# Loading half of a weight by a pattern of eight: fused cross-covariance attention and mixture-of-depths MLP

## The chip, the cores and the metric

The kernel runs on one core of one Trainium2 chip. The metric is the device time of one execution in microseconds (us); the median of three runs before the change is 258.89 us (258.16 to 259.0). A core has TensorE (PE, with its weight loads PEld), VectorE (DVE), ScalarE (ACT), GpSimd (POOL), SyncE (SP), and sixteen DMA engines that move data between HBM and the on-chip memory SBUF. SBUF has 128 partitions. Matmuls write to PSUM.

## The reference

Two stages, for four batches of N = 6208 tokens with C = 256 channels, all float32:

```python
qn = q / (norm(q, axis=1) + 1e-6)            # over the tokens
kn = k / (norm(k, axis=1) + 1e-6)
a  = softmax(kn^T @ qn / tau)                # 256 x 256 per batch
x  = v @ a
scores = x @ w_gate                          # one per token
idx    = the 128 tokens of a batch with the highest scores
h  = relu(x[idx] @ w1)                       # w1: 256 x 1024
ye = h @ w2                                  # w2: 1024 x 256
out = x;  out[idx] = x[idx] + sigmoid(scores[idx]) * ye
```

The 1024 columns of w1 and the 1024 rows of w2 are the MLP's units. A unit is column i of w1 and row i of w2; in which order the units are summed doesn't matter, as long as both weights use the same order.

## The kernel before

**Tiles and order.** A batch is cut into six chunks of 1024 tokens (8 rows on each of 128 partitions) and a rest of 64 tokens. For each batch the kernel loads the q and k chunks, then the v chunks. GpSimd issues these loads (lines 187 and 189, in `emit_load`); they are cast to bf16 on the way, so a load of 1 MB from HBM fills 512 KB of SBUF. Per q/k chunk TensorE adds to three accumulators: k^T q (line 303) and the Gram matrices of q and of k (lines 305 and 307). At the end of a batch's q and k come the norms and the softmax; then v is transposed (line 403), the scores are formed (line 440), and the output is formed (line 474), copied to a staging buffer (line 482, ScalarE) and stored by SyncE (line 491, in `emit_store`, 1 MB per chunk). The selection of 128 tokens is a search for a threshold on VectorE. The selected rows of v are gathered by an indirect DMA (line 603), run through attention and MLP again (`h_ps` line 646, `y_ps` line 660), and scattered over the output (line 697).

**What sets the order.** The program writes the order of the work out by hand. While it is built, a planner keeps a clock per engine (`vt_clock`) and a model of the two DMA queues (`Rings`), and at each step picks what is ready: a step of a selection or MLP chain, a score, an output, or the next input row. Loads are issued by `pump` as buffers come free, at most four not yet landed by the planner's model. On the chip each engine works through its instructions in the order written and waits on semaphores.

**The DMA queues.** GpSimd's loads go through a software queue (q0 in the profile), SyncE's weights and stores through a hardware queue (q1). Both are served by the same sixteen engines. A DMA of 128 partitions is dealt out over the sixteen, eight partitions to each. When an engine has done its share it writes a 4-byte packet, the completion; a load has landed when all sixteen are there.

**The weights (lines 215 to 226 and 845 to 854).** At the start SyncE loads w1 and w2 in float32 into two of the staging buffers, `w1_st` and `w2_st`, and the gate's vector into `wg_row`. Partition p of `w2_st` gets the eight rows 8p to 8p+7 of w2, so w2's unit order is "unit 8p + fc is row p of block fc". ScalarE casts both to bf16, and the cast of w1 sorts its columns into the same blocks:

```python
nc.sync.dma_start(out=w2_st, in_=moe_w2.rearrange("(p fc) d -> p fc d", p=P))
...
w1v = w1_st.rearrange("p a c -> p (a c)").rearrange("p (dc m fc) -> p dc fc m", dc=C // P, fc=NFC)
for dc in range(C // P):
    nc.scalar.copy(w1_sb[:, dc, :].rearrange("p (fc m) -> p fc m", fc=NFC), w1v[:, dc])
nc.scalar.copy(w2_sb, w2_st)
```

Then a small matmul and a copy spread the gate's vector over the partitions (lines 850 to 852). w1 and w2 are first used by the MLP of the first batch; w2 also serves as operand of matmuls that only keep TensorE busy (`idle`, line 841).

Of the kernel before, what the change touches and what calls it, by code (L numbers as in the profile page):

```python
# [18 lines left out]
P = 128  # L19
# [8 lines left out]
def kernel(  # L28
# [12 lines left out]
    nc = tc.nc  # L41

    B, N, C = q.shape
# [6 lines left out]
    NFC = F // P  # L50
# [101 lines left out]
    def now():  # L152
        return vt_clock["pe"]
# [49 lines left out]
    def pump():  # L203
        rings.run(now())
        flying[:] = [key for key in flying if rings.done.get(key, 1.0e9) > now()]
        while nxt_unit[0] < len(units):
            u = units[nxt_unit[0]]
            if in_use[bucket(u)] >= limit[bucket(u)] or len(flying) >= AHEAD:
# [6 lines left out]
    w1_sb = const.tile([P, C // P, F], BF16)  # L215
# [3 lines left out]
    w1_st = st_pool.tile([P, RPP, C], F32, name="stage")  # L219
    w2_st = st_pool.tile([P, RPP, C], F32, name="stage")  # L220
    nc.sync.dma_start(out=w1_st.rearrange("p a c -> p (a c)").rearrange("p (dc f) -> p dc f", dc=C // P),
                      in_=moe_w1.rearrange("(dc p) f -> p dc f", p=P))
    nc.sync.dma_start(out=w2_st, in_=moe_w2.rearrange("(p fc) d -> p fc d", p=P))
    nc.sync.dma_start(out=wg_row, in_=moe_w_gate[None, :])
    rings.add(1, 2.0, UNIT, "w1")
    rings.add(1, 2.7, UNIT, "w2")
# [566 lines left out]
    def stage_ready():  # L793
        if len(stage_keys) < ST_BUFS:
            return 0.0
        key = stage_keys[-ST_BUFS]
        if key in stage_free:
            return stage_free[key]
        return rings.landing(("st",) + key) + 0.3
# [43 lines left out]
    while True:  # L843
        pump()
        if not cast_done and now() > 8.0:
            w1v = w1_st.rearrange("p a c -> p (a c)").rearrange("p (dc m fc) -> p dc fc m", dc=C // P, fc=NFC)
            for dc in range(C // P):
                nc.scalar.copy(w1_sb[:, dc, :].rearrange("p (fc m) -> p fc m", fc=NFC), w1v[:, dc])
            nc.scalar.copy(w2_sb, w2_st)
            wg_ps = ps_m.tile([P, 512], F32, name="m_ps")  # L850
            nc.tensor.matmul(wg_ps[:, 0:C], lhsT=ones_f[0:1, :], rhs=wg_row, start=True, stop=True)
            nc.scalar.copy(wg_bcast, wg_ps[:, 0:C])
            vt_clock["act"] = max(vt_clock["act"], now()) + 4.5
            cast_done = True
# [9 lines left out]
        if eat_at < len(eat):  # L864
            kind, u, x = eat[eat_at]
            if u in loaded:
                row = x if kind == "p1" else x[1]
                r = rings.landing(arrival_key[u + (int(row >= RPP // 2),)]) + 0.1
                if acc_dead[0]:
                    r += -0.7 if u == ("v", L, LAST) else 0.7  # L870
                if kind == "p1":
                    if u[2] == FIRST and x == 0:
                        r = max(r, acc_free[0])
                else:
                    r = max(r, min(vt_bank)) if vt_live < VT_BUFS or acc_dead[0] else FAR
# [5 lines left out]
        if out_at < len(outs):  # L881
            b, g, pr = outs[out_at]
            if b in a_ready and (b, g) in vts and score_at > gs.index(g) + b * len(gs) and (
                    (b, g[0]) not in late or hot):
                r = max(a_ready[b], vt_ready[(b, g)], min(o_bank))
                if g[0] < NFULL and g[1] == 0 and pr == 0:
                    r = max(r, stage_ready())
                if eat_at < len(eat) and eat[eat_at][0] == "p1" and b == E and r < t + 1.0:
                    arr = able[-1][0] if able and able[-1][1] == 2 else FAR
                    if max(r, t) < arr < max(r, t) + 0.5:  # L890
                        r = FAR
# [10 lines left out]
        if fit:  # L902
            r, prio, what = min(fit, key=lambda a: (a[1], a[0]))
# [5 lines left out]
        else:  # L909
            r, prio, what = min(able, key=lambda a: (a[0], a[1]))  # L910
# [122 lines left out]
```

## Time and profile before

| | |
|---|---|
| median of 3 runs | 258.89 us (258.16 to 259.0) |
| the profiled execution | 257.59 us, its span 255.9 us |
| granted TensorE clock, mean | 0.977 of full |
| PE busy | 214.0 us (84%) |
| PEld busy | 187.4 us (73%) |
| ACT busy | 106.5 us (42%) |
| DVE busy | 92.4 us (36%) |
| POOL busy | 56.9 us (22%) |
| HBM read, written | 78.91 MB, 25.95 MB: 410 GB/s over the span |
| chain that ended last | DMA 60%, PE 26%, issue 4%, DVE 4% |

The span runs from the first to the last instruction; the rest of an execution's time lies around it (1.7 us here). Busy shares are means over the whole span. The chain that ended last is followed back from the last instruction, at each step to what released it.

### The profile page before, as it was taken

The numbers are of one execution on the slowest core, as the hardware profiler recorded it, in microseconds if no ns is written. First come the engines' busy times: TensorE is split into PE (matmuls) and PEld (weight loads), VectorE is DVE, ScalarE is ACT, GpSimd is POOL, SyncE is SP. The second block draws the span as 40 slices with busy tenths as digits, with TensorE's granted clock in tenths as the row PEclk, the third lists the DMA queues.
The fourth block names the chain that finished last, engine by engine and source line by source line (L and its number), as shares of the span: only waits on it lengthen the run. The fifth ranks groups of instructions, "written<-read, shape, count | busy, mean of one in ns | idle before, by whom it ended". The sixth has DMA issues, their size and how long they took to land.

```text
span 255.9 us, 6666 instructions
## 1 busy us (share of the span) xinstructions
PE 214.0 (84%) x2878; PEld 187.4 (73%) x2878; DVE 92.4 (36%) x409; ACT 106.5 (42%) x186; POOL 56.9 (22%) x106
## 2 busy tenths in 40 slices
PE   0099877899999539989999789899999999999960
PEld 0069767798878539878888678788898878888840
DVE  2000001725552002545645006546751064488130
ACT  3800002754554102584234005774313069697740
POOL 7323110522005100722201404112313310000301
PEclk9999999999999958999999999999999999999996
DMA  6999999999999999999999999999999999999996
GB/s 240 258 216 215 214 214 211 215 207 247 272 318 316 315 295 213 224 215 211 264 279 254 214 210 214 213 272 308 219 213 219 214 209 239 415 423 406 376 425 252
DMA packets 17903, 66.88 MB, mean 261 GB/s; under 512 B 2129, under 2 KB 3666, under 8 KB 15058
## 3 DMA queue, kind: packets, MB, share of 16 engines
q0 software_dynamic: 12672, 38.93, 76.4%
q1 hardware_dynamic: 5202, 27.53, 26.7%
q8 instruction: 22, 0.36, 0.5%
q14 instruction: 7, 0.06, 0.1%
HBM read 78.91 MB, written 25.95 MB: 410 GB/s over the span
## 4 chain that ended last, share of the span: by engine, by line
DMA 60%; PE 26%; issue 4%; DVE 4%; POOL 2%; ACT 1%; POOLq 1%; DVEq 0%
DMA k_ch<-in_k_dram 40%; DMA q_ch<-in_q_dram 17%; PE s_ps L303 4%; PE o_ps L474 4%; PE vt_ps L403 4%; DMA out_dram<-stage 3%; PE g_ps L307 2%; PE g_ps L305 2%; PE sc_ps L440 2%; PE g_ps L474 2%; PE s_ps L474 1%; PE o_ps L841 1%; POOL q_ch L187 1%; PE m_ps L550 1%; ACT e L357 1%
## 5 line engine op out<-in xcount | busy, mean ns | idle before, releaser
L303 PE MATMUL s_ps<-q_ch,k_ch 128*128 128x256 bf16 x384 | 90.6, 280 | 27.8 <-DMA k_ch<-in_k_dram 27.8
L305 PE MATMUL g_ps<-q_ch 128*128 128x128 bf16 x384 | 85.8, 224 | 0.0
L307 PE MATMUL g_ps<-k_ch 128*128 128x128 bf16 x384 | 85.8, 223 | 0.0
L482 ACT COPY stage<-o_ps 128x512 f32<-128x512 f32 x77 | 43.9, 589 | 44.0 <-PE o_ps L474 41.7
L303 PEld LDWEIGHTS <-k_ch 128*128 128x128 bf16 x384 | 38.4, 100 | 30.6 <-DMA k_ch<-in_k_dram 29.8
L307 PEld LDWEIGHTS <-k_ch 128*128 128x128 bf16 x384 | 38.6, 100 | 5.4
L305 PEld LDWEIGHTS <-q_ch 128*128 128x128 bf16 x384 | 38.4, 100 | 0.1
L474 PE MATMUL o_ps<-a_sb,vt_sb 128*128 128x256 bf16 (+1 forms) x250 | 35.5, 272 | 1.0 <-ACT stage L482 0.5
L317 DVE CUSTOM_DVE_ANT_0 junk<-g_ps,ident_f 128x128 f32<-128x128 f32 x16 | 4.7, 291 | 67.4 <-PE g_ps L307 67.0
L474 PEld LDWEIGHTS <-vt_sb 128*128 128x128 bf16 (+1 forms) x264 | 23.7, 97 | 6.6 <-issue 3.3
L403 PE MATMUL vt_ps<-ident_b,v_ch 128*128 128x128 bf16 x360 | 25.4, 219 | 2.8 <-ACT vt_sb L417 2.5
L403 PEld LDWEIGHTS <-v_ch 128*128 128x128 bf16 x384 | 23.2, 97 | 5.1 <-issue 3.9
L313 ACT COPY s_sb<-s_ps 128x512 f32<-128x512 f32 x4 | 2.3, 586 | 56.5 <-PE s_ps L303 56.5
L187 POOL DMA_DIRECT2D v_ch<-in_v_dram x26 | 14.2, 547 | 45.2 <-PE vt_ps L403 18.2
L417 ACT COPY vt_sb<-vt_ps 128x1024 bf16<-128x1024 bf16 (+1 forms) x26 | 22.6, 927 | 2.9 <-PE vt_ps L403 2.9
L187 POOL DMA_DIRECT2D q_ch<-in_q_dram x25 | 13.9, 557 | 29.6 <-DMA q_ch<-in_q_dram 10.0
L841 PE MATMUL o_ps<-w_sb,ident_b 128*128 128x256 bf16 x124 | 18.8, 272 | 0.2 <-ACT h_sb L651 0.2
L187 POOL DMA_DIRECT2D k_ch<-in_k_dram x25 | 13.6, 543 | 23.6 <-DMA v_ch<-in_v_dram 9.6
L603 POOL DMA_INDIRECT vg<-in_v_dram,idx x4 | 4.0, 1008 | 63.2 <-DVE idx L599 33.8
L534 DVE SCALAR_TENSOR_TENSOR cmp<-sc,wl,tab 128x392 bf16<-128x392 f32 x28 | 17.5, 626 | 1.0
L841 PEld LDWEIGHTS <-ident_b 128*128 128x128 bf16 x124 | 10.7, 97 | 1.3 <-issue 0.4
L553 DVE TENSOR_REDUCE cnt<-m_ps 128x8 f32<-128x56 f32 x28 | 6.1, 216 | 15.3 <-PE m_ps L550 14.9
(189 smaller groups left out, 270.7 us busy)
## 6 DMA issues: line engine op xcount, KB each, us to landing
out_dram<-stage SPq DMA_DIRECT2D x21, 1024.0 KB, 10.6
q_ch<-in_q_dram POOLq DMA_DIRECT2D x23, 512.0 KB, 17.2
k_ch<-in_k_dram POOLq DMA_DIRECT2D x23, 512.0 KB, 18.8
v_ch<-in_v_dram POOLq DMA_DIRECT2D x22, 512.0 KB, 14.8
stage<-in_moe_w_dram SPq DMA_DIRECT2D x2, 1024.0 KB, 7.0
out_dram<-stage SPq DMA_DIRECT2D x8, 256.0 KB, 8.1
v_ch<-in_v_dram POOLq DMA_DIRECT2D x4, 256.0 KB, 11.2
out_dram<-stage SPq DMA_DIRECT2D x2, 512.0 KB, 5.3
```

What stands on the lines that cost most here:

```text
L187: ins = nc.gpsimd.dma_start(out=t[:, rows, :], in_=view(src, b, ci)[:, rows, :])
L303: nc.tensor.matmul(s_ps[:, cc, :], lhsT=ks[:, sl], rhs=qs, start=begin and cc == 0, stop=end and cc == 1)
L305: nc.tensor.matmul(g_ps[:, cc, :], lhsT=qs[:, sl], rhs=qs[:, sl], start=begin and cc == 0, stop=False)
L307: nc.tensor.matmul(g_ps[:, 2 + cc, :], lhsT=ks[:, sl], rhs=ks[:, sl], start=False, stop=end and cc == 1)
L403: nc.tensor.transpose(vt_ps[:, cc, j, :parts], in_=vt[:parts, s0 + j, cc * P:(cc + 1) * P], identity=ident_b[:parts, :parts])
L417: nc.scalar.copy(vt_sb[:, :, :n, :parts], vt_ps[:, :, :n, :parts])
L440: nc.tensor.matmul(sc_ps[:parts, first + j, :], lhsT=vt_sb[:, cc, j, :parts], rhs=aw_sb[:, cc, :], start=begin and cc == 0 and j == 0, sto ...
L474: nc.tensor.matmul(o_ps[:parts, pj, :], lhsT=vt_sb[:, cc, j, :parts], rhs=a_sb[:, cc, :], start=pj == 0 and cc == 0, stop=pj == m - 1 and ...
L482: nc.scalar.copy(st[:parts, s0 + pair * 2:s0 + pair * 2 + m, :], o_ps[:parts, :m, :])
L534: nc.vector.scalar_tensor_tensor(out=cmp, in0=sc[:, 0:NCOL, None].to_broadcast([P, NCOL, NTHR]), scalar=wl[:, i, NTHR:NTHR + 1], in1=tab[: ...
L553: nc.vector.tensor_reduce(out=cnt9[:, 0:NTHR], in_=mps[:, 0:7 * NTHR].rearrange("p (s j) -> p j s", s=7), axis=AX.X, op=ALU.add)
L841: nc.tensor.matmul(o_ps[:, 0, :], lhsT=ident_b, rhs=w2_sb[:, 0, :], start=True, stop=True)
```

## The change

w2 is loaded by two DMAs. Rows 64 to 127 of the view of w2 as 128 rows of 8 KB go to partitions 64 to 127 as before. Rows 0 to 63 go to partitions 0 to 63 in another order: the HBM side is a pattern of three dimensions, outermost a = 8 (step one row), then r = 8 (step eight rows), then the row's 2048 numbers. Partition 8a + r receives row 8r + a. So in the lower half the units stand in another order, and the cast of w1 sorts its columns in the same way, with two casts for each half of w1's rows in place of one (lower and upper half of the partitions' units).

```diff
-    nc.sync.dma_start(out=w2_st, in_=moe_w2.rearrange("(p fc) d -> p fc d", p=P))
+    HP = P // 2
+    w2_rows = moe_w2.rearrange("(j fc) d -> j (fc d)", fc=NFC)
+    nc.sync.dma_start(out=w2_st[HP:P].rearrange("p a c -> p (a c)"), in_=w2_rows[HP:P])
+    nc.sync.dma_start(out=w2_st[0:HP].rearrange("p a c -> p (a c)"),
+                      in_=w2_rows[0:HP].rearrange("(r a) x -> a r x", a=8))
     nc.sync.dma_start(out=wg_row, in_=moe_w_gate[None, :])
...
-            w1v = w1_st.rearrange("p a c -> p (a c)").rearrange("p (dc m fc) -> p dc fc m", dc=C // P, fc=NFC)
+            w1v = w1_st.rearrange("p a c -> p (a c)").rearrange("p (dc h m fc) -> p dc h fc m", dc=C // P, h=2,
+                                                                fc=NFC)
+            w1o = w1_sb.rearrange("p dc (fc h m) -> p dc h fc m", fc=NFC, h=2)
             for dc in range(C // P):
-                nc.scalar.copy(w1_sb[:, dc, :].rearrange("p (fc m) -> p fc m", fc=NFC), w1v[:, dc])
+                low8 = w1v[:, dc, 0].rearrange("p fc (r a) -> p fc a r", a=8)
+                nc.scalar.copy(w1o[:, dc, 0].rearrange("p fc (a r) -> p fc a r", a=8), low8)
+                nc.scalar.copy(w1o[:, dc, 1], w1v[:, dc, 1])
             nc.scalar.copy(w2_sb, w2_st)
```

The planner's model of the queues still counts w2 as one load of 2.46 us.

## Rows read from the trace of the kernel before

**Rows 1.** Table by stretches: us, busy us (instructions) per engine, granted clock, DMA share, GB/s
```profile
13.00:40.00 27.00, 22.50 (x251) 19.41 (x252) 0.00 (x0) 0.37 (x1) 5.85 (x11) 1.00 1.06 213
...
217.00:235.00 18.00, 17.90 (x262) 15.09 (x259) 12.38 (x49) 14.62 (x29) 0.00 (x0) 1.00 1.02 415
...
243.00:253.20 10.20, 4.43 (x47) 3.23 (x44) 2.55 (x8) 2.66 (x6) 0.97 (x1) 0.90 1.01 420
```

**Rows 2.** Timeline of PE: start, us; in brackets idle before and its releaser
```profile
29.19 0.28 PE L303 MATMUL s_ps<-q_ch,k_ch 128*128 128x256 bf16 x1 [1.13 <-DMA k_ch<-in_k_dram]
...
93.45 0.39 PE L303 MATMUL s_ps<-q_ch,k_ch 128*128 128x256 bf16 x1 [6.23 <-DMA k_ch<-in_k_dram]
...
151.17 0.28 PE L303 MATMUL s_ps<-q_ch,k_ch 128*128 128x256 bf16 x1 [1.17 <-DMA k_ch<-in_k_dram]
...
197.33 0.28 PE L303 MATMUL s_ps<-q_ch,k_ch 128*128 128x256 bf16 x1 [0.33 <-DMA k_ch<-in_k_dram]
...
203.07 0.28 PE L303 MATMUL s_ps<-q_ch,k_ch 128*128 128x256 bf16 x1 [0.27 <-DMA k_ch<-in_k_dram]
```

**Rows 3.** End of the chain that ended last (start, us), and POOL's last instruction
```profile
240.66 8.53 DMA out_dram<-stage
...
250.34 0.97 POOL L697 DMA_INDIRECT out_dram<-upd,idx  x1 [9.85 <-DMA out_dram<-stage]
```

**Rows 4.** DMA packets in 22.45:23.05, 207.0:207.5, 208.64:208.66, 208.95:209.4 and 210.05:210.35, in order
```profile
DMA packets 47, 0.13 MB, mean 212 GB/s; under 512 B 16, under 2 KB 16, under 8 KB 47
...
DMA packets 36, 0.12 MB, mean 238 GB/s; under 512 B 7, under 2 KB 7, under 8 KB 36
...
DMA packets 5, 0.02 MB, mean 819 GB/s; under 512 B 1, under 2 KB 1, under 8 KB 5
...
DMA packets 32, 0.11 MB, mean 237 GB/s; under 512 B 6, under 2 KB 6, under 8 KB 32
...
DMA packets 25, 0.07 MB, mean 218 GB/s; under 512 B 2, under 2 KB 2, under 8 KB 25
```

**Rows 5.** DMA queues, whole span: packets, MB, share of 16 engines
```profile
q1 hardware_dynamic: 5202, 27.53, 26.7%
q8 instruction: 22, 0.36, 0.5%
```

**Rows 6.** Timeline of the start, and SP's next issue
```profile
1.32 0.45 SPq L223 DMA_DIRECT2D stage<-in_moe_w_dram  x1
...
1.81 0.34 SPq L224 DMA_DIRECT2D wg_row<-in_moe_w_gate_dram  x1
...
5.72 3.95 ACT L848 CAST w_sb<-stage 128x1024 bf16<-128x1024 f32 x2 [3.63 <-DMA stage<-in_moe_w_dram]
...
13.21 0.39 PE L303 MATMUL s_ps<-q_ch,k_ch 128*128 128x256 bf16 x1 [13.21 <-DMA k_ch<-in_k_dram]
...
43.40 0.59 ACT L313 COPY s_sb<-s_ps 128x512 f32<-128x512 f32 x1 [27.60 <-PE s_ps L303]
...
58.96 0.37 SPq L491 DMA_DIRECT2D out_dram<-stage  x1
```

**Rows 7.** DMA issues: KB each, median us from issue to landing (missing here)
```profile
wg_row<-in_moe_w_gate_dram SPq DMA_DIRECT2D x1, 1.0 KB
```

**Rows 8.** Packets in 1.90:2.02, 2.02:2.20, 2.20:2.34, 4.90:5.10; q1's in 9.56:9.76, 10.04:10.05
```profile
DMA packets 8, 0.03 MB, mean 273 GB/s; under 512 B 0, under 2 KB 0, under 8 KB 8
...
DMA packets 0, 0.00 MB, mean 0 GB/s; under 512 B 0, under 2 KB 0, under 8 KB 0
...
DMA packets 13, 0.05 MB, mean 380 GB/s; under 512 B 0, under 2 KB 0, under 8 KB 13
...
DMA packets 27, 0.11 MB, mean 533 GB/s; under 512 B 7, under 2 KB 7, under 8 KB 21
...
q1 hardware_dynamic: 7, 0.00, 4.8%
...
q1 hardware_dynamic: 1, 0.00, 36.9%
```

## The prediction

> **What bounds the kernel now.** I read the table by stretches first, then the waits on TensorE, the DMA packets in short windows, and the end of the chain of waits. In [rows 1] the reader is to see a DMA share of 1.06 from 13 to 40 us, 1.02 from 217 to 235 and 1.01 from 243 to 253 (over 1 because packets of one engine overlap a little): the sixteen DMA engines work without a break, loads first, stores last. TensorE is full only between 217 and 235 (17.90 of 18 us). In [rows 2] it waits for a K chunk time after time, the last two times at 197.33 (0.33 us) and at 203.07 (0.27 us); after that no matmul waits for a load. So the time is set by the load stream up to 203 us, by TensorE's own work up to about 241, and by the stores that have piled up from there ([rows 3]: the last store on the chain is issued at 240.66 and takes 8.53 us; the scatter waits 9.85 us for stores).
>
> A load is complete when the last of its sixteen engines is. What matters is therefore not what the engines move together but what the slowest has had to do. [rows 4] shows the sixteen completion packets (4 bytes, the "under 512 B" column) of one load at two ages of the program. At 22.5 us all sixteen come within 0.6 us. For a V load at 207 us they come in four clusters: seven by 207.5, one at 208.65, six between 208.95 and 209.4, two after 210.05. Seven engines have kept pace; eight are 2 to 3 us behind; one stands between. The difference is not in the data, which every load deals out evenly. [rows 5] gives a cause: 22 instruction packets of 16 KB on q8. 0.5% of 16 x 255.9 us is 20.5 us, so 0.93 us each. Six engines late by two of them (1.9 us) and two late by three (2.8 us) use up 18 of the 22, which is how many would be due at 207 us if they are spread over the span (22 x 207/256). So the fetches fall on eight engines only, in turn. That those eight are always the same is my reading of the clusters, and of the packet records followed from one packet of an engine to the next; no row names an engine.
>
> **The change part by part.** *The load.* Before, the second weight (1 MB, the second SP issue in [rows 6]) gives each engine 64 KB. Now 64 of its rows (512 KB) are still spread over sixteen, 32 KB each. The other 64 rows have an outermost dimension of eight on the HBM side. If the DMA is split by that dimension, eight engines get 64 KB more and eight get nothing: 96 KB against 32 KB where all had 64. The nearest row for the price is the hardware queue's own line in [rows 5]: 26.7% of 16 x 255.9 us is 1093 us for 27.53 MB, 39.7 us per MB, so 32 KB is 1.30 us. Eight engines run 1.3 us later from about 12 us on, eight run 1.3 us earlier, and since no engine is idle before 203 us, the offset lasts.
>
> *Does it split so, and which eight?* The trace has one DMA with an outermost dimension under sixteen: wg_row, one row of 1 KB. It is the one line among the DMA issues without a landing time [rows 7], and one packet of the hardware queue starts in 10.04 to 10.05 [rows 8]: it used one engine. Which one? The first weight starts in two bursts: eight packets in 1.90 to 2.02, then none until 2.20, where the other eight engines begin (13 packets by 2.34, five of them second packets of the first eight). Seven engines then finish it by 5.10, and the second weight's completions show seven again in 9.56 to 9.76 [rows 8]. wg_row's packet comes 0.3 us, one packet, after one of those seven; followed packet by packet it is on an engine of the first burst, and the first four instruction fetches all fall on engines of the second burst. The first burst's eighth member starts late and is the one between the clusters. I take it that the eight engines of the first burst are the eight that a short outermost dimension selects. Then the extra 1.3 us goes to the engines without fetches.
>
> The Trainium skill, "DMA: Bandwidth & Descriptors", section "Why a DMA increments its semaphore by 16 and not by 1", says that the number of engines is the largest up to 16 that divides the slowest dimension of both sides, and that SP's queue takes the lowest-numbered; for 64 and 8 that is eight. The wg_row packet agrees as to the count; no row shows numbers.
>
> *The sum.* Apply it to the V load of [rows 4]: the seven move from 207.5 to 208.8, the one from 208.65 to 209.95, the eight from 210.3 to 209.0. The last completion moves from 210.25 to 209.95: 0.3 us earlier. The full 1.3 us isn't had, because the engine in between becomes the last one. TensorE can use it: 0.33 us of waiting at 197.33 and 0.27 us at 203.07, together 0.6 us, bound what it can take. Then the stores: eight engines balanced against eight let the pile of 243 to 253 us end nearer to its mean. With a spread of 2 to 3 us between the clusters at 207, part of which goes as early engines run dry between stores, I put this at between 0 and 0.6 us and take 0.15, near the low end, because the engine in between stays late. Together 0.45 us.
>
> *What hides the rest.* In the first 25 us there is no lag to remove, so the first K chunk lands some 1.3 us later and TensorE starts at about 14.5 instead of 13.21 [rows 6]. That is covered by its wait of 1.13 us at 29.19 and of 1.17 us at 151.17 [rows 2]; without those it would cost 1.3 us. Around 83 to 93 us, where loads and stores share the engines, the in-between engine can land a load up to 1 us later; the wait of 6.23 us at 93.45 then grows, TensorE's work behind it is late by as much, and later waits such as the one at 151.17 take it back. *ScalarE.* Two casts of 1024 columns (3.95 us, 1.97 each, [rows 6]) become four of 512: between 3.95 us and, if each strided one costs as much as a whole one, 7.9 us; I take 4.4. The second weight's cast starts about 1.3 us later. ScalarE's next work after the gate row is at 43.40, after 27.60 us idle: nothing. *SP.* One issue more, some 0.45 us (the spacing of 1.32 and 1.81), and wg_row behind it; SP's next issue is at 58.96 [rows 6]. *The units' new order* adds no instruction on TensorE: both weights are permuted alike. The staging buffers of the weights come free a little later, long before the first store at 58.96: nothing.
>
> The profiled execution took 257.59 us, 1.3 under the median of 258.89. 257.59 - 0.45 is 257.1; from the median it is 258.4, which I forecast.
>
> **The rivals.** *The wrong eight (slower).* The same split, but the eight include engines that take the fetches. Then the latest two of [rows 4] come at 211.6 instead of 210.3, the wait at 197.33 grows by 1.3 us and everything behind it follows: 258.9 + 1.3 = 260.2. It decides as soon as two engines with fetches are among the eight. For it: nothing in the trace names engines, and the packet-by-packet reading is delicate. Against: wg_row's engine is in the first burst. The Trainium skill speaks for this side: the same page, "Rules for kernel authors", wants an outermost dimension that is a multiple of 16, since a smaller one confines the whole DMA to that many engines. By that rule alone this edit is a loss of the extra 1.3 us; the rows agree with the rule only where all engines are equally late, as at 22.5 us.
>
> *The full balance.* If the in-between engine's lag is not its own but passes about, or it catches up while stores run, the loads end 1.3 us earlier: 258.9 - 1.3 = 257.6. For it: the lag at 207 of 1.5 us is not a round number of fetches, and several waits before 203 would each give some back. Against: TensorE's own work from 203 on takes only 0.6 us of it.
>
> *No split.* The load goes over sixteen engines after all (the two 8s are one run of 64 rows on the SBUF side): nothing moves, 258.9.
>
> **How the numbers follow.** Two runs of this kernel are told apart from about 0.3%, 0.78 us. Forecast 0.55; full balance 0.20; wrong eight 0.15; no split 0.10. The forecast's own range is 257.9 to 258.9. Faster by over 0.78 us: most of the full balance (0.18) and a sixth of the forecast (0.09), 0.27. Slower: most of the wrong eight (0.14) and a little of the forecast (0.02), 0.16. Same: the rest, 0.57. The range reaches to 257.5, under the full balance, and to 259.9, almost to the wrong eight, so that about 2 in 10 is left out.
>
> **What would show it.** Right: a DMA issue of the second weight without a landing time; completions of early loads (22 us) in two clusters of eight, 2.6 us apart; late ones (207 us) within 2 us with one straggler; TensorE's first matmul at about 14.5; the last wait for K at 203 smaller. Wrong: early loads still within 0.6 us (no split), or late ones spread over 4 us (wrong eight). A gain over 1 us would say that the in-between engine doesn't matter or that the store stage gains more than I gave it.

## The result and the profile after

The changed kernel takes 261.12 us (median of six runs, 260.26 to 262.46), the kernel before 258.68 us (six runs, 257.71 to 259.86). The ratio is 1.010, with a 95% interval of 1.0056 to 1.0145: slower, by about 2.4 us. The profiled execution took 260.39 us, its span 258.7 us, at a granted clock of 0.978 (before: 0.977).

The first view is TensorE's timeline, with the rows that answer to [rows 2] and to the first matmul of [rows 6].

```profile
16.50 0.40 PE L309 MATMUL s_ps<-q_ch,k_ch 128*128 128x256 bf16 x1 [16.50 <-DMA k_ch<-in_k_dram]
...
31.57 0.28 PE L309 MATMUL s_ps<-q_ch,k_ch 128*128 128x256 bf16 x1 [0.29 <-DMA k_ch<-in_k_dram]
...
97.24 0.40 PE L309 MATMUL s_ps<-q_ch,k_ch 128*128 128x256 bf16 x1 [4.57 <-DMA k_ch<-in_k_dram]
...
154.01 0.28 PE L309 MATMUL s_ps<-q_ch,k_ch 128*128 128x256 bf16 x1 [1.17 <-DMA k_ch<-in_k_dram]
...
200.24 0.28 PE L309 MATMUL s_ps<-q_ch,k_ch 128*128 128x256 bf16 x1 [0.28 <-DMA k_ch<-in_k_dram]
...
205.56 0.28 PE L309 MATMUL s_ps<-q_ch,k_ch 128*128 128x256 bf16 x1
```

Read the starts against [rows 2]: 13.21 has become 16.50 (+3.3), 29.19 has become 31.57 (+2.4), 93.45 has become 97.24 (+3.8), 151.17 has become 154.01 (+2.8), 203.07 has become 205.56 (+2.5). All of the loss is there with the first chunk; on the way it moves between 2.4 and 3.8 us, and at 203 us 0.8 us of the first 3.3 has been given back. Now read the brackets: the wait at 154.01 is 1.17 us, exactly as it was at 151.17. It was to take lateness back and took none.

The end answers to [rows 3]: the chain's last store and the last scatter start 2.4 and 2.6 us later; the store takes 8.88 us instead of 8.53.

```profile
243.02 8.88 DMA out_dram<-stage
...
252.98 0.97 POOL L703 DMA_INDIRECT out_dram<-upd,idx  x1 [10.00 <-DMA out_dram<-stage]
```

Why is the first chunk late? The completion packets (the "under 512 B" column) of the K load that [rows 4] shows within 0.6 us at 22.5 come in two clusters of eight, in 21.8 to 22.2 and in 25.6 to 26.35:

```profile
DMA packets 28, 0.08 MB, mean 205 GB/s; under 512 B 8, under 2 KB 8, under 8 KB 28
...
DMA packets 50, 0.17 MB, mean 229 GB/s; under 512 B 8, under 2 KB 8, under 8 KB 50
```

By their first records (21.90 and 25.65) the clusters are 3.8 us apart, where 2.6 was forecast. And they don't lie evenly about the old time: the early eight are 0.7 us earlier, the late eight 3.2 us later. The reason is in the hardware queue's line (packets, MB, share of sixteen engines) while the second weight moves. First the kernel before, 6 to 10 us:

```profile
q1 hardware_dynamic: 107, 0.75, 46.8%
```

Then the changed kernel, upper half (6.3 to 8.2 us) and lower half (9 to 13 us):

```profile
q1 hardware_dynamic: 34, 0.27, 55.3%
...
q1 hardware_dynamic: 41, 0.34, 35.0%
```

Share times 16 engines times the stretch, over the MB, is the price that the prediction took from [rows 5] as 39.7 us per MB. Before it is 0.468 x 64 / 0.75 = 39.9. After it is 0.553 x 30.4 / 0.27 = 62 in the upper half and 0.350 x 64 / 0.34 = 66 in the lower one. So the shares are uneven, and the packets of both halves also cost, on average, 1.6 times as much: some 0.5 us per 8 KB instead of 0.32.

### The profile page after: what moved, and what is told of

It is laid out like the page before. It is cut to its first block, busy times and chain, and to the rows that moved or that the text cites. A ratio compares the mean times of both kernels' runs of the same rounds, so it can differ in the third digit from the quotient of the medians.

```text
span 258.7 us, 6671 instructions
## 1 busy us (share of the span) xinstructions
PE 214.8 (83%) x2878; PEld 187.9 (73%) x2878; DVE 92.5 (36%) x409; ACT 106.6 (41%) x188; POOL 56.8 (22%) x106
## 4 chain that ended last, share of the span: by engine, by line
DMA 63%; PE 21%; issue 5%; POOL 4%; DVE 3%; POOLq 1%; ACT 0%; DVEq 0%
DMA k_ch<-in_k_dram 43%; DMA q_ch<-in_q_dram 10%; DMA q_rem<-in_q_dram 7%; PE s_ps L309 5%; DMA out_dram<-stage 3%; PE o_ps L480 3%; PE g_ps L313 2%; PE g_ps L311 2%; PE vt_ps L409 2%; POOL q_ch L187 2%; PE g_ps L480 2%; PE s_ps L480 1%; PE sc_ps L446 1%; POOL k_ch L187 1%; POOL v_ch L187 1%
## 5 line engine op out<-in xcount | busy, mean ns | idle before, releaser
L309 PE MATMUL s_ps<-q_ch,k_ch 128*128 128x256 bf16 x384 | 91.7, 282 | 29.5 <-DMA k_ch<-in_k_dram 29.3
## 6 DMA issues: line engine op xcount, KB each, us to landing
v_ch<-in_v_dram POOLq DMA_DIRECT2D x22, 512.0 KB, 14.5
```

Of the source, the lines that this page charges most:

```text
L309: nc.tensor.matmul(s_ps[:, cc, :], lhsT=ks[:, sl], rhs=qs, start=begin and cc == 0, stop=end and cc == 1)
```

## The experiments

Sixteen runs were made, of fourteen kernels (one was profiled three times), each beside the kernel before on the same chip. K "of 203 us" is the chunk whose use is the last row above. An engine's share of the second weight was 64 KB (2.60 us at 39.7 us per MB, twice the prediction's 1.30 us for 32 KB); the changed kernel deals out 96 and 32 KB. The expectations name their theories by letters. A: eight engines have more to do, and how late they are is the cost. B: loads into 64 partitions have dear packets. C: the first batch's scatter holds up the loads behind it. D: a stray delay that every kernel has. E: TensorE's low clock behind its long waits.

### Which part of the change costs: casts, halves, or eight engines

**The casts alone.**

```diff
-    nc.sync.dma_start(out=w2_st[HP:P]..., in_=w2_rows[HP:P])          # changed kernel
-    nc.sync.dma_start(out=w2_st[0:HP]..., in_=w2_rows[0:HP].rearrange("(r a) x -> a r x", a=8))
+    nc.sync.dma_start(out=w2_st, in_=moe_w2.rearrange("(p fc) d -> p fc d", p=P))
```

> The load of before with the four casts of the changed kernel (the MLP's units then don't match: only the time is meant). Theories A and B: 258.7, as before. A third one, that the casts or the order of units cost: up to 261.

Measured: 257.89 us, ratio 0.9999 (0.9982 to 1.0017). The four casts cost nothing that can be seen.

**Two halves, all sixteen engines.**

```diff
-    nc.sync.dma_start(out=w2_st, in_=moe_w2.rearrange("(p fc) d -> p fc d", p=P))
+    for h in (1, 0):
+        nc.sync.dma_start(out=w2_st[h * HP:(h + 1) * HP]..., in_=w2_rows[h * HP:(h + 1) * HP])
```

> The second weight in two plain halves of 64 partitions, each spread over all sixteen engines; unit order and casts as before. Theory A (the eight engines' extra load is what costs): nothing to see, all completions of a load at 22 us within 0.6 us, 258.7. Theory B (a transfer confined to 64 partitions moves its packets slower, 520 to 600 ns instead of 322, on however many engines): both halves have slow packets, 8 x 0.2 us = 1.6 us later on every engine at 22 us, no two clusters; the time between 259.5 and 260.5.

**The lower half as two loads of 32 partitions,** each with its own outermost eight, so that an engine writes four neighbouring partitions of each.

```diff
-    nc.sync.dma_start(out=w2_st[0:HP]..., in_=w2_rows[0:HP].rearrange("(r a) x -> a r x", a=8))
+    for g in range(2):
+        blk = slice(32 * g, 32 * g + 32)
+        nc.sync.dma_start(out=w2_st[blk]..., in_=w2_rows[blk].rearrange("(r a) x -> a r x", a=8))
```

> As the changed kernel, but the lower half goes in two loads of 32 partitions, each with eight outermost members; so each of the eight engines writes only four neighbouring partitions of each block. Theory A: as the changed kernel, 261, clusters 3.8 us apart at 22 us. Theory B in the form that two engines then write the same group of partitions in the changed kernel: the lower half's packets take 322 ns again, the clusters are 2.6 us apart, time 259.5 to 260.3.

**Halves again, but every other row of HBM.**

```diff
-    nc.sync.dma_start(out=w2_st, in_=moe_w2.rearrange("(p fc) d -> p fc d", p=P))
+    w2_rows = moe_w2.rearrange("(j h fc) d -> h j (fc d)", h=2, fc=NFC)
+    for h in (1, 0):
+        nc.sync.dma_start(out=w2_st[h * HP:(h + 1) * HP]..., in_=w2_rows[h])
```

> The second weight as two loads of 64 partitions, each on all sixteen engines, as in e1_halves, but each half takes every other row of 8 KB, so that both loads read over the whole 1 MB in HBM; the cast of the first weight sorts the units accordingly. Theory B1 (a load confined to 64 partitions is slow, wherever it reads): packets of 8 KB take 520 to 620 ns as in e1_halves, first matmul at 15.0 to 15.5, time 259.0 to 259.6 beside a before of 257.8 to 258.0. Theory B2 (a contiguous half of 512 KB in HBM is slow to read): packets take the usual 322 ns, first matmul at 13.2 to 13.6, time as before, 257.8 to 258.3.

Measured: the two halves 259.29 us, ratio 1.0044 (1.0021 to 1.0067); the blocks of 32 259.07 us, 1.0043 (1.0021 to 1.0065); every other row 259.79 us beside 258.65, 1.0033 (0.9996 to 1.007), first matmul at 14.70. The first two are just under theory B's ranges, which begin at 259.5. For every other row the interval includes no change, so there the price and the first matmul (13.21 before) have to tell. The hardware queue's line for the two halves (6 to 12 us):

```profile
q1 hardware_dynamic: 119, 0.79, 60.3%
```

For every other row (6 to 11 us):

```profile
q1 hardware_dynamic: 109, 0.76, 62.2%
```

And for the blocks of 32, while the lower half moves (9 to 13 us):

```profile
q1 hardware_dynamic: 58, 0.41, 25.3%
```

That is 73, 65 and 39 us per MB. A load into 64 partitions is dear on all sixteen engines, wherever it reads in HBM; into blocks of 32 by eight engines, with rows of 8 KB, it has its old price. The number of engines doesn't decide: the changed kernel's lower half, eight engines on 64 partitions, was dear too (66). So the cause lies on the SBUF side of the load. The Trainium skill, "SBUF — State Buffer", section "Door 1: The DMA port swizzle (why `[64,N]` ≈ `[32,N]`)", says that 64 partitions in one half of the SBUF reach only eight of its sixteen ports; sixteen engines would then share eight, and eight engines on a block of 32 would have one each. The three prices agree with that; no row names a port. The 66 of the changed kernel's lower half doesn't follow from the count alone, by which eight engines would have eight ports; whether two of them use one port at the same time, no row shows.

### Which share costs: eight engines with more, no load into a half

All 128 partitions by sixteen engines for the first F0 of each partition's eight rows, the other rows by four loads of 32 partitions on eight engines: F0 = 4 gives the shares of the changed kernel (+-32 KB), F0 = 6 half as much.

```diff
-    nc.sync.dma_start(out=w2_st, in_=moe_w2.rearrange("(p fc) d -> p fc d", p=P))
+    nc.sync.dma_start(out=w2_st[:, 0:F0, :], in_=moe_w2.rearrange("(p fc) d -> p fc d", p=P)[:, 0:F0, :])
+    for g in range(4):
+        blk = slice(32 * g, 32 * g + 32)
+        nc.sync.dma_start(out=w2_st[blk, F0:NFC, :]...,
+                          in_=w2_rows[blk, F0 * C:].rearrange("(r a) x -> a r x", a=8))
```

> The same with half of the second weight (four of the eight rows of each partition): eight engines +32 KB, eight -32 KB, the shares of the changed kernel, with no load of 64 partitions. Theory B: first matmul at 14.5 as the prediction had it, clusters 2.6 us apart at 22 us, and the time is the prediction's sum, 257.5 to 258.0 beside a before of 258.0. Theory A: the waits that the prediction counted on don't take it back; 258.8 to 259.3, the first matmul at 14.5 and the K chunk of 93 us some 1.3 to 2.6 us later.

> A quarter of the second weight (two of the eight rows of each partition) goes to eight engines, through four loads of 32 partitions with an outermost dimension of eight; three quarters go as one load of all 128 partitions over sixteen engines. No load is confined to 64 partitions. Eight engines get 16 KB more than before, eight 16 KB less: +-0.65 us by the prediction's price. Theory B (all the loss comes from slow packets of loads of 64 partitions): packets of the second weight take their usual time, first matmul at 13.2 to 13.9, and the time is 257.7 to 258.2, as before or slightly better, as the prediction's sum wants. Theory A (unequal shares cost by themselves): completions at 22 us in two clusters some 1.3 us apart and 258.4 to 258.7. The unknown is the smaller packets (2 KB rows twice per partition); if these are slow, the first matmul tells (over 14.5).

Measured: F0 = 4 260.40 us beside 257.81, ratio 1.0094 (1.0076 to 1.0111), the loss of the changed kernel without a load into a half. F0 = 6 258.86 us, 1.0031 (1.0016 to 1.0046). Both are slower than theory A's own ranges. With F0 = 4 the first matmul starts at 14.30, where the prediction had 14.5, and yet the time is 2.6 us up. It is not a test of the forecast's 1.3 us, though: the second weight is still on its way then (31 packets of the hardware queue, 0.09 MB, start between 14.4 and 15.6 us), its rows of 4 KB have a dear price of their own (55 us per MB, 9 to 15 us), and the slowest engine ends up 2.5 us late. The lateness is all there by 24 us. The issues of the third Q load (KB, us from issue to landing; all are issued at 6.76 or 6.77), for the kernel before:

```profile
q_ch<-in_q_dram POOLq DMA_DIRECT2D x1, 512.0 KB, 14.1
```

For the changed kernel:

```profile
q_ch<-in_q_dram POOLq DMA_DIRECT2D x1, 512.0 KB, 17.4
```

For F0 = 4, the two halves, and the blocks of 32:

```profile
q_ch<-in_q_dram POOLq DMA_DIRECT2D x1, 512.0 KB, 16.6
```

```profile
q_ch<-in_q_dram POOLq DMA_DIRECT2D x1, 512.0 KB, 16.0
```

```profile
q_ch<-in_q_dram POOLq DMA_DIRECT2D x1, 512.0 KB, 15.8
```

The slowest engine's lateness there, and the time against the kernel before: 3.3 and 2.4 us (changed kernel), 2.5 and 2.6 (F0 = 4), 1.9 and 1.3 (two halves), 1.7 and 1.1 (blocks of 32). For F0 = 6 the K load issued behind it (at 7.28 and 7.29) tells, in the kernel before and with F0 = 6:

```profile
k_ch<-in_k_dram POOLq DMA_DIRECT2D x1, 512.0 KB, 16.0
...
k_ch<-in_k_dram POOLq DMA_DIRECT2D x1, 512.0 KB, 16.9
```

That is 0.9 us late, and 1.05 us lost in the median. What the slowest engine loses in the first 20 us, the kernel loses, less at most 0.9 us: theory A. The lateness follows roughly from the prices: 96 KB at 62 to 66 us per MB is 6.1 to 6.5 us instead of 2.60, +3.5 to 3.9 (changed kernel, measured 3.3); 64 KB at 73 is 4.8, +2.2 (two halves, 1.9); 32 KB at 39.7 and 64 KB at 55 are 4.9, +2.3 (F0 = 4, 2.5).

### What carries the lateness through: three suspects behind it

In the changed kernel the engines stand idle for a while (share of sixteen engines, the last column but one, 104 to 110 us; the kernel before has 1.07 there):

```profile
104.00:110.00 6.00, 6.00 (x80) 5.48 (x78) 2.10 (x12) 1.65 (x3) 2.48 (x4) 1.00 0.85 174
```

0.22 of 6 us is 1.3 us of all sixteen. The first batch's scatter is issued late and holds up the loads behind it in GpSimd's queue. **Scatter behind five more loads,** in the changed kernel, the kernel before and the blocks of 32:

```diff
-            return max(rings.landing(key) for key in stored[b]) + 3.0
+            return max(rings.landing(key) for key in stored[b]) + (20.0 if b == 0 else 3.0)
```

> The changed kernel with the first batch's scatter put five loads later in GpSimd's queue. Theory C (the landing that is 3.8 us later at 93 us delays the first batch's update, and the scatter that waits for it holds up the loads behind it, so that the fast engines run dry around 105 us): no dry time at 105 to 109, 259.0 to 260.0. If the loss is already complete at 93 us: 261.

> The kernel before, with the first batch's scatter moved behind five more loads in GpSimd's queue (as in the earlier run of the changed kernel with that move). It is the control for that move. If the hold-up of loads behind the scatter (theory C) costs nothing where no engine has run dry by 105 us, the time is that of the kernel before, 258.0 +- 0.5. If the move itself costs something (the MLP's buffers come free later, the output rows of the first batch are held longer), it is slower by up to 1 us, and the run of the changed kernel with the move has hidden a gain of that size.

> The low half as two loads of 32 partitions with an outermost dimension of eight, as in e2_own (259.07, 1.1 us over before), and the scatter moved as in e5. Theory C (the eight early engines run dry at 105 to 108 us because loads queue behind the scatter): no dry time there, and 0.5 to 1.1 us of the loss is recovered: 258.0 to 258.6. Theory A (the uneven shares cost by themselves: the eight late engines land every load later, whatever the others do) and theory B (the upper half's packets are slow): unchanged, 259.1 +- 0.4.

Measured: changed kernel 260.92 us beside 258.00, 1.0117 (1.008 to 1.0155); kernel before 257.95, 0.9996 (0.9976 to 1.0016); blocks of 32 259.11, 1.0046 (1.0028 to 1.0065). The idle stretch is gone in the changed kernel:

```profile
104.00:110.00 6.00, 6.00 (x80) 5.47 (x78) 2.13 (x12) 1.59 (x3) 0.32 (x1) 1.00 1.07 215
```

and nothing is gained, in the blocks of 32 either. Those who stood idle were the early engines: in the changed kernel the completions of a V load that begins to land at 102.5 us are spread over 5.3 us, those of a Q load at 124.0 over 1.7. Theory C falls.

**The same kernel in two groups.** Executions of F0 = 6 fell into five at 257.8 to 258.5 and seven at 258.8 to 259.5, so it was profiled twice more.

> The kernel of e7_cols6 once more, for another profile: its executions fell in two groups, five at 257.8 to 258.5 and seven at 258.8 to 259.5, and the profile showed one of the first group, where no time is lost (last wait for K at 203.13 against 203.07). If the upper group is the unequal shares at work (theory A), a profile of that group shows loads that land late on the eight engines with more to do, or engines standing idle at 104 to 112 us as in e8_cols4, and the K chunk of 203 us about 1.3 us later. If it is something else that no share explains (theory D: a stray delay that every kernel has), the loads up to 203 us land as in the first profile and the time is lost behind them.

> The same kernel a third time, since which group an execution falls into can't be chosen. Theory A: in the upper group the K chunk of 203 us lands 1.0 to 1.5 us later than in the lower one, with the DMA engines idle at 104 to 112 us. Theory D: the loads land alike in both groups.

They took 258.91 and 259.45 us (first profile: 257.93), on a chip where the kernel before took 258.65 instead of 257.81, so that what tells is inside the traces. All three begin alike: the K load of 7.3 us takes 16.9, 17.1 and 17.0 us to land. Scatter issue and two stretches (clock in the third column from the right) of the first profile:

```profile
98.00:101.00 3.00, 3.00 (x47) 2.90 (x46) 0.86 (x3) 1.06 (x3) 0.00 (x0) 0.98 1.06 213
104.00:110.00 6.00, 5.99 (x78) 5.26 (x76) 3.50 (x19) 3.48 (x5) 4.19 (x9) 1.00 1.06 221
...
103.28 1.01 POOL L703 DMA_INDIRECT out_dram<-upd,idx  x1 [12.53 <-DVE upd L671]
```

and of the third:

```profile
98.00:101.00 3.00, 3.00 (x24) 2.57 (x22) 0.86 (x3) 0.37 (x1) 0.00 (x0) 0.50 1.06 214
104.00:110.00 6.00, 6.00 (x80) 5.45 (x78) 2.48 (x14) 2.38 (x4) 3.23 (x6) 1.00 0.90 175
...
104.97 1.01 POOL L703 DMA_INDIRECT out_dram<-upd,idx  x1 [14.14 <-DVE upd L671]
```

The K chunk of 93 us was used 0.3 us apart (94.94 and 95.27). But after that wait (4.89 us in the one, 6.53 in the other) TensorE ran at 1.2 GHz until about 98.1 us in the one and 101.2 in the other, with 47 and 24 matmuls in the same 3 us; the scatter is 1.7 us later, the engines idle, K of 203 us is used at 203.13 and 204.65. The second profile has the scatter at 103.30 and the full clock from 98 to 101, but its clock fell again later:

```profile
149.30:152.30 3.00, 3.00 (x24) 2.54 (x23) 0.00 (x0) 0.00 (x0) 0.53 (x1) 0.50 1.10 210
```

From 149 to 153 us the other two have it at 1.00. In the second profile K of 203 us is used at 204.11. So the two executions with more time at 1.2 GHz are late at 203 us, and the one without is not, although its slowest engine had been 0.9 us late: at this dose the waits could take the lateness back. Three executions suggest that; they don't prove it.

**TensorE kept at work in its waits** (theory E): matmuls on data at hand in front of the K chunks of 85 to 88 and 93 to 97 us.

```diff
+            if s == 0 and (u[1], u[2]) in FILL:
+                o_ps = ps_o.tile([P, 2, C], F32, name="o_ps")
+                for i in range(FILL[u[1], u[2]]):
+                    nc.tensor.matmul(o_ps[:, 0, :], lhsT=ident_b, rhs=w2_sb[:, 0, :], start=True, stop=True)
             p1_row(u[1], u[2], s)
```

> The kernel before with 48 matmuls of 256 columns (on data at hand, result unused) in front of the K chunk of 93 us, where TensorE waits 6.23 us: some 5.2 us of work at the high clock. It is the control. Theory E: the chunk's matmuls and the first MLP behind it run at 2.4 GHz from the start instead of 1.2 GHz from 93.45 to 97.6; in 4.1 us at half speed TensorE lost some 2 us, so the K chunk of 141 us is used as soon as it lands, and the scatter of 102.22 is issued at about 100.3; time as before or up to 0.7 us faster (257.1 to 257.9), since the loads of 141 us and later bound TensorE anyway. Theory A: no change, 257.8 +- 0.3.

> The kernel of e7_cols6 (eight engines +16 KB) with 16 such matmuls in front of the K chunk of 85 us and 40 in front of that of 93 to 95 us. Theory E: no low clock at 95 to 101 us, scatter issued by 102, no idle engines at 104 to 110 us, and the upper group of executions goes: median 257.5 to 258.1 instead of 258.86. Theory A: two groups as before, median 258.6 to 259.1.

> The changed kernel with 20 such matmuls in front of the K chunk of 87.7 us and 36 in front of that of 97.2 us. Theory E: the low clock of 97 to 101 us (and that of 88 to 90) goes, the scatter is issued at about 104 instead of 105.70, the engines stand idle for less, and of the loss of 2.4 us 1 to 1.8 us come back: 258.6 to 260.0. Theory A: what the first loads lost is lost: 260.6 to 261.3.

Measured: kernel before 257.84 beside 258.21, 0.9984 (0.9963 to 1.0005); F0 = 6 258.30, 1.0008 (0.999 to 1.0026), ten of twelve executions up to 258.6; changed kernel 261.35, 1.0124 (1.0095 to 1.0154). For the small dose the loss can't be told from none any more, though its interval overlaps that without the fill (1.0016 to 1.0046): the low clock seems to have a part in this loss, how large stays open. The execution profiled with the fill (258.10 us) uses K of 203 us at 204.31 nevertheless, behind a later stretch at a low clock (0.72 granted from 164 to 170 us), so lateness at 203 us and the time don't always go together. In the changed kernel the fill was short: 2.31 us of the wait were left and the clock fell behind it all the same, so this run tells nothing. With more matmuls, without and with the late scatter:

> The changed kernel with 22 matmuls in front of the K chunk of 87.6 us and 58 (6.2 us) in front of that of 97.2 to 97.5 us, so that TensorE has at most 0.3 us without work before it. Theory E: clock at 2.4 GHz throughout 88 to 104 us, scatter issued at 104.5 instead of 105.7 to 106.0, the idle stretch of 104 to 110 us shorter by about 1 us, and 0.5 to 1 us come back: 260.1 to 260.7. Theory A: the lateness of the slowest engines alone sets the time: 261 to 261.5 as before.

> The same with the first batch's scatter moved behind five more loads in GpSimd's queue. Theory E: neither low clock nor idle engines; what remains is what the slow packets of the two halves cost, 1.2 to 1.5 us of all engines: 259.0 to 259.7. Theory A: the slowest eight engines are 3.2 us late from the start and nothing makes up for it: 260.5 to 261.3.

Measured: 260.98 us beside 258.13, 1.0107 (1.0085 to 1.013), and 261.39, 1.0133 (1.0105 to 1.0161). The last one's stretches and its K of 203 us:

```profile
97.00:104.00 7.00, 7.00 (x95) 6.62 (x93) 1.79 (x7) 1.55 (x4) 1.05 (x2) 1.00 1.07 213
104.00:110.00 6.00, 6.00 (x82) 5.46 (x80) 2.57 (x17) 2.66 (x4) 1.35 (x3) 1.00 1.07 214
...
205.28 0.28 PE L309 MATMUL s_ps<-q_ch,k_ch 128*128 128x256 bf16 x1
```

Clock full, no engine idle, and the K chunk is nearly as late as in the changed kernel (205.56). The second time is far above what theory E had for it (259.0 to 259.7), the first a little (260.1 to 260.7). Theory E falls for the changed kernel, theory A stands: the lateness of the slowest eight alone is enough. What the early engines did with their lead is no matter to the time: in this run the sixteen completions of that K load are spread over 5.3 us, in the changed kernel, where the early ones stood idle, over 2.6, and the last ones are 0.3 us apart (205.23 and 205.51). A late landing also makes the next issue late. The K load of 203 us is issued 3.8 us later than before, in both kernels as soon as an earlier Q load has landed (the kernel before first):

```profile
189.31 0.53 POOL L187 DMA_DIRECT2D k_ch<-in_k_dram  x1 [1.91 <-DMA q_ch<-in_q_dram]
...
193.09 0.53 POOL L187 DMA_DIRECT2D k_ch<-in_k_dram  x1 [1.93 <-DMA q_ch<-in_q_dram]
```

No kernel of the study is shown to beat the kernel before.

## Why the prediction was wrong, point by point

- **The split into eight, and which eight: right.** Two clusters of eight, and the lower half's issue has no landing time. The instruction fetches still fall on the other eight: in the changed kernel's K load that lands at 36.41, seven completions come in 32.03 to 32.26, one at 33.24, all in the early cluster.
- **"32 KB is 1.30 us": the term that was mis-sized.** The slowest engines lost 3.2 to 3.3 us. At the old price 1.3 of that is the share; the two halves with even shares lost 1.9 by themselves. The sum took the price per MB from loads of 128 partitions and gave it to loads of 64, which cost 1.6 to 1.8 times as much. No row of before showed a large load into 64 partitions, and the sum had no upper bound for it.
- **"The last completion moves 0.3 us earlier": failed.** K of 203 us landed 2.5 us later. The sum moved the three kinds of engine by 1.3 us each way; with 3.2 one way and 0.7 the other, the engines without fetches became the last. The lead of the others was no use either: in the changed kernel they spent most of it standing idle around 105 us.
- **"Covered by its wait", "later waits take it back": failed.** Of the first 3.3 us the waits gave back 0.8. Of those named, the one at 29.19 shrank from 1.13 to 0.29 and that of 151.17 stayed 1.17; that of 93.45 went from 6.23 to 4.57, but the one 10 us before it grew from 0.33 to 2.86. A wait for a load isn't slack when the load is what is late: the K chunks of 146 and 151 us are used 4.87 us apart in both kernels (146.30 and 151.17, then 149.14 and 154.01), at the pace of their loads. And a late landing holds up the next issue, as the two issues above show. Whether the waits would have covered the 1.3 us that the sum had, no run shows. F0 = 4 had 2.5 us. F0 = 6 had 0.9 to 1.1, of which one profile took everything back by 203 us and two did not.
- **"TensorE is full only between 217 and 235": misread.** Between 151.17 and 197.33 no matmul waits for K, and TensorE is busy for 14.98 of the 15 us from 182 to 197. In the changed kernel the same way takes as long (154.01 to 200.24). On that stretch there is no wait for a load that could give anything back; TensorE's own work carries the lateness on.
- **Casts at nothing: right** (ratio 0.9999). The extra issue and the new order of the units have no run of their own.
- **The rivals.** "The wrong eight" had the nearest time (260.2) and the right sign, but not the mechanism: the eight were those without fetches. The rule that spoke for it (the Trainium skill, "DMA: Bandwidth & Descriptors", section "Rules for kernel authors", on an outermost dimension below 16) was right in its direction. F0 = 4, with no load into a half, bears it out: 1.0094. "Full balance" would have needed the lateness of 22 us to be of no account.
- **What would show it.** The late completions of the 207 us loads were to come within 2 us with one straggler; they are spread over 2.7 us, without clusters. The wait at 203 went (0.27 to none) because TensorE itself came late, 2.9 us at the chunk before it.

## What to carry over

In a kernel whose DMA engines never rest, add up each engine's time, not the load's: the slowest engine's loss in the first 20 us was the kernel's here, less at most 0.9 us, and TensorE's waits for those same loads are little cover for it. Take the price of a load from a row with the same partitions: half of the partitions cost far more than half of the time (62 to 73 us per MB against 40). To even out the engines, the gift should be smaller than the lead that the receivers have at that moment, and at the start they have none; no run here tried a later gift.

## What the hardware showed that was not expected

- A load of 512 KB into 64 partitions took 62 to 73 us of engine time per MB, one into 128 took 40, and loads of 32 partitions by eight engines took 39 (8 KB rows) to 55 (4 KB rows, 9 to 15 us with F0 = 4; what made some of these slow isn't settled).
- After waits of 4.89 and 6.53 us TensorE was granted 1.2 GHz, and went on at it for 3.2 us of unbroken work in one execution and 6.0 in another of the same kernel; a third had its second low stretch at 149 us. At half speed the difference is 1.4 us, about the distance between the two groups of executions; that it is the cause of the groups isn't shown.
